# Crossbar transposes in an attention and channel-mix kernel: outputs of batches 4 to 7 pair by pair, q and k of batches 4 and 5 as well

## Chip, cores and metric

One core of one Trainium2 chip. The metric is device time in microseconds; the time before is 234.25 us, the median of three runs (233.97 to 234.29).

## The reference

Sliding-window attention with a linear distance bias over 8 batches of 8 heads (576 positions, 64 per head), then a channel mix of the attention's output with its own row before. Cut to what is computed:

```python
# q, k, v: (8, 8, 576, 64)
scores = q @ k.T / sqrt(64)
rel = i - j                       # query less key position
scores = where((rel >= 0) & (rel < 128), scores - slope[h] * abs(rel), -1e9)
attn = softmax(scores) @ v
x = attn.transpose(0, 2, 1, 3).reshape(8, 576, 512)

x_prev = x shifted down by one row (a zero row first)
xk = mu_k * x + (1 - mu_k) * x_prev
xr = mu_r * x + (1 - mu_r) * x_prev
k = relu(xk @ w_k)                # w_k: 512 x 1024
v = (k * k) @ w_v                 # w_v: 1024 x 512
out = sigmoid(xr @ w_r) * v       # w_r: 512 x 512
```

## The kernel before

The kernel doesn't call its instructions in the order in which they run. It describes each piece of work as a node with an engine, an assumed duration, its dependences, a priority and the buffers that it takes and frees; a list scheduler (`Plan.run`) then plays the program through with these durations and fixes the order on every engine. On the chip each engine runs its list in order and waits by semaphores. The scheduler also has a make-believe engine FAB, which stands for the DMA engines: `dma` and `fab` cut a transfer into pieces of about 0.25 us there, and their `lat` gives the time from issue to the first piece and from the last piece to the landing. None of these numbers is in the program itself; they set its order.

Heads go in pairs: batch b has four pairs g = 0 to 3, each 128 wide (two heads of 64). A pair passes these stations:

- Loads on GpSimd's queue, which cast to bf16: q and k into `cb` (L471, two buffers), the last 64 positions of q and k into `ts` (L461), v into `vs` and `tv`. A load waits until its buffer is free.
- q and k with the head dimension on partitions. Batches 3 to 5 do that on TensorE, two pairs at a time: `qk_some` (L1153) with 32 transposes of 64 columns (L779), and copies by ScalarE from PSUM to `qk`. Batches 1 and 2 have a like form (L1032). For batches in `XB`, which are 6 and 7, the crossbar of the DMA does it: `flip` (L474) issues eight transposes per batch on SyncE's queue (SP), each 128 x 512 from `cb` to one of two `qx` buffers. `XTT` (batches 4 to 7) does the same for the tails, `tail_flip` (L564), from `ts` to `tt`.
- Scores on TensorE (L666), exponential on ScalarE (L680), mask on VectorE (L693).
- Attend on TensorE (L724), then reciprocal (L730) and normalisation (L735) on VectorE, which writes the pair's output in bf16: to `xu` (one of three buffers), or for batches in `XO` (6 and 7) to `xb`, which holds all four pairs of a batch.
- The output with the channel on partitions, in `xt`. `out_t` (L751) does it with five TensorE transposes (L762) and one ScalarE copy. For batches in `XO`, `out_flip` (L841) waits for all four pairs and issues five crossbar transposes on SP (L847), one for each 128 positions.
- `shift` (L805) on VectorE: the difference of a row and the one before into `dl` (L822), and the two mixes xk and xr (L829).

Every one or two batches `channel_mix` (L922) takes xk and xr in column blocks of 512, 384 or 256: TensorE multiplies by `w_k` (L937), ScalarE takes relu (L944), VectorE squares (L910), TensorE multiplies by `w_r` (L955) and `w_v` (L971), VectorE multiplies the two (L976) into `ot`, and SP stores it (L1001). These blocks are laid between the attention's pieces and fill TensorE.

SP's queue holds in one order: the output stores, the tail transposes, the q and k transposes, the output transposes. An instruction that waits holds up those behind it.

Of the kernel before, what the change touches and what calls it, by code (L numbers as in the profile page):

```python
# [10 lines left out]
BF16 = mybir.dt.bfloat16  # L11
# [168 lines left out]
def kernel(  # L180
# [12 lines left out]
    nc = tc.nc  # L193

    B, H, S, D = q.shape
# [13 lines left out]

    PE, ACT, DVE, POOL, SPE, FAB, VIR = "PE", "ACT", "DVE", "POOL", "SP", "FAB", "VIR"  # L210
    NQ, NA, NX, NV, NC = 4, 4, 3, 2, 2
    XB = range(6, B)
    XO = range(6, B)
    X0 = 16
    NWARM = 90
    LOADS = 'vK23tVkabRcWw'
# [7 lines left out]
    TW = (0,)  # L224
    QUAD = 0.040
    RUN = {2: 64 * 284 / 345.0, NF: 128 * 284 / 390.0}
    FLIP = 1.25
    NO = 5
    WAIT = 1.0
    QM = 2  # L230
# [26 lines left out]
    def many(n, shape, dtype, name):  # L257
        return [cst.tile(shape, dtype, name=f"{name}{i}") for i in range(n)]
# [16 lines left out]
    at_buf = many(NA, [128, 2 * 1024 + 64], BF16, "at")  # L275
    rc_buf = many(NX, [128, 2, NJ], FP32, "rc")
    xu_buf = many(NX, [128, NJ, 2, D], BF16, "xu")
    xb_buf = many(2, [128, NJ, H, D], BF16, "xb")
    xt_buf = many(2, [128, NPO, X0 + S], BF16, "xt")
    dl_buf = many(2, [128, S], BF16, "dl")  # L280
    xk_buf = many(2, [128, NPO, SP], BF16, "xk")
    xr_buf = many(2, [128, NPO, SP], BF16, "xr")
# [25 lines left out]
    def two(h):  # L308
        return duo[h.idx]

    plan = Plan(dict(qx=2, xb=2, p2=2, p1=N1, pt=4 - N1, qk=NQ, at=NA, xu=NX, vs=NV, cb=NC, ts=2, tt=2, xt=2, dl=2, dl0=4,
                     xk=2, rl=3, kk=3, rs=4, ot=NO),
                {}, WAIT)
    LAT = {PE: 0.2, ACT: 0.22, DVE: 0.16}
# [36 lines left out]
    def virtual(key, holds):  # L351
        n = plan.add(VIR, 0.0001, 0.0001, [last.get(key)], (0,), None, holds)
        last[key] = n
        return n
# [117 lines left out]
            out=cb_buf[h.idx][:, i, r], in_=src[:, :, r]), [g]) for r in range(NF)]  # L472

    def flip(b, i, j, g):  # L474
        return dma(SPE, FLIP * RATE, 1.3, lambda e: nc.sync.dma_start_transpose(
            out=qx_buf[xbh[b].idx][:, i, :, 128 * j:128 * j + 128],
            in_=cb_buf[ch[b].idx][:, i, j].rearrange("p h d -> p (h d)")),
            [g, (cl[b][NF * i + j], 6.0)], (), [ch[b]])

    def w_load(dst, src, kb):  # L480
        return dma(POOL, kb, 0.85, lambda e: nc.gpsimd.dma_start(
# [82 lines left out]
    def tail_flip(b):  # L564
        htt, hs = Hold("tt"), th[b]
        g = plan.add(VIR, 0.0001, 0.0001, [], (0,), None, [htt])
        tth[b], ttg[b] = htt, g
        ttl[b] = [dma(SPE, FLIP * RATE, 1.3, lambda e: nc.sync.dma_start_transpose(
            out=tt_buf[htt.idx][:, :, 0:2].rearrange("p g t c -> p g (t c)"),
            in_=ts_buf[hs.idx].rearrange("p h d -> p (h d)")),  # L570
            [g] + [(x, 6.0) for x in tl[b]], (), [hs])]

    def batch_load(b, what):
        if what == "a":
# [124 lines left out]
    def attend(b, g, t0, t1, ha, deps, prio):  # L699

        nt = t1 - t0
        n_mm = sum(2 if t > 0 else 1 for t in range(t0, t1)) * 2
        hp, hx = Hold("p1" if 2 * nt * W <= 512 else "p2"), xbh_o[b] if b in XO else Hold("xu")
        rc = rc_buf[(4 * b + g) % NX]

        def xo():
            if b in XO:
                return xb_buf[hx.idx][:, t0:t1, 2 * g:2 * g + 2]
            return xu_buf[hx.idx][:, t0:t1]
        hv = vh[b]  # L710

        def a5():
            if hp.cls == "p1":
                return one(hp)[:, 0:2 * nt * W].rearrange("p (h t c) -> p h t c", h=2, c=W)
            return two(hp)[:, :, 0:nt * W].rearrange("p h (t c) -> p h t c", c=W)

        def emit(e):
            at, vs, tvb, a = at_buf[ha.idx], vs_buf[hv.idx], tv_buf[hv.idx], a5()
            for t in range(t0, t1):
                for hl in range(2):  # L720
                    us = [u for u in (t - 1, t) if u >= 0]
                    for u in us:
                        lo = 1024 * hl + BASE[u] + 128 * (t - u)
                        nc.tensor.matmul(  # L724
                            a[:, hl, t - t0], lhsT=at[:, lo:lo + 128],
                            rhs=vs[:, u, 2 * g + hl, :] if u < NF else tvb[:, 2 * g + hl],
                            start=(u == us[0]), stop=(u == t), skip_group_check=True)

        def emit_r(e):
            nc.vector.reciprocal(out=rc[:, :, 0:nt], in_=a5()[:, :, :, D])  # L730

        def emit_x(e):
            out_ = xo().rearrange("p t h d -> p h t d")
            if e == DVE:
                nc.vector.tensor_tensor(  # L735
                    out=out_, in0=a5()[:, :, :, 0:D],
                    in1=rc[:, :, 0:nt, None].to_broadcast([128, 2, nt, D]), op=ALU.mult)
                return
            for t in range(nt):
                for hl in range(2):  # L740
                    nc.scalar.activation(out=out_[:, hl, t], in_=a5()[:, hl, t, 0:D],
                                         func=AF.Copy, scale=rc[:, hl, t:t + 1])

        a = op(PE, 0.029 * n_mm, deps, prio + (0,), emit, [hp], [ha, hv])
        r = op(DVE, 0.2, [a], prio + (0,), emit_r)
        on = XU(b, g)
        r = op(on, {ACT: 0.197 * 2 * nt, DVE: dve_t(2 * nt * D)}, [r], prio + (0,), emit_x,
               [] if b in XO else [hx], [hp])
        return r, hx

    def out_t(b, g, t0, t1, hx, deps, prio, hk, ht, late=None):  # L751
# [86 lines left out]
                res.append(mix())  # L838
        return res

    def out_flip(b, rs, hx, ht):  # L841

        res = []
        for t in range(NJ):
            rows = min(128, S - 128 * t)
            n = plan.add(SPE, 1.3 * rows / 128, 0.0, rs + [virt_xt[b]], (0, len(plan.nodes)),
                         lambda e, t=t, rows=rows: nc.sync.dma_start_transpose(  # L847
                out=xt_buf[ht.idx][:, :, X0 + 128 * t:X0 + 128 * t + rows],
                in_=xb_buf[hx.idx][0:rows, t].rearrange("p h d -> p (h d)")))
            res.append(fab(SPE, 1.0 * rows / 128, n, (1.0, 0.9), [hx]))  # L850
        return res

    def tails_full(b, prio, htt, hs):
        hp = Hold("p1")
# [45 lines left out]

    of = out.rearrange("b s m -> (b s) m")

    n_hw = 39 + sum(4 if g in FT else 2 for g in range(3)) + 8 * len(XB) + len(XTT) + NJ * len(XO)
    n_split = -n_hw % 8

    def square(e, out, in_):
# [99 lines left out]

    xh, virt_x, virt_xt, xth, xbh_o = {}, {}, {}, {}, {}

    def begin(b):
        if b % 2 == 0:
# [181 lines left out]
    for b in range(1, B):  # L1194
        begin(b)
        P = b // 2
        rs = []
        if b in XO:
            xbh_o[b] = Hold("xb")
            rs.append(virtual("xb", [xbh_o[b]]))  # L1200
        htt, n_tt = tails(b, (0, b, 0, 0))
        for g in range(G):
            prio = (0, b, 0, g)
            ha = Hold("at")
            if b in XB:
                hq, y = xbh[b], xbl[b]
                pace = paced(b, g)
            else:
                pace = []
                if b in WIDE:  # L1210
                    two_q[:] = [qk_quad(b, g, NF, lambda b=b: wide_buf[ch[b].idx], cw[b][g // 2] + paced(b, g),
                                        prio, 0, Hold("qk"), True, [ch[b]])]
                elif not QM:
                    two_q[:] = [qk_full(b, g, prio)]
                elif g % QM == 0:
                    two_q[:] = qk_some(b, g, QM, prio)
                hq, y = two_q[0 if b in WIDE else g % max(QM, 1)]
            _, (m0, m1) = scores(b, g, [HALF0 + (None,), HALF1 + (htt,)], 4 * b + g < NBIAS, hq, ha,
                                 y + pace + (n_sid if b < 3 else []) + n_tt, prio, [ha], [hq, htt])
            r, hx = attend(b, g, 0, NJ, ha, [m0, m1] + vl[b] + rs[0:1], prio)  # L1220
            if b in XO:
                rs.append(r)
            elif not OM:
                xks[b, g], xrs[b, g] = out_t(b, g, 0, NJ, hx, [r], prio, xh[P], xth[b])
            else:
                two_x.append((hx, r))
                if len(two_x) < OM:
                    continue
                xs = out_some(b, g - OM + 1, [x for x, _ in two_x], [x for _, x in two_x], prio, xth[b])
                two_x.clear()  # L1230
                for j in range(g - OM + 1, g + 1):
                    xks[b, j], xrs[b, j] = shift(b, j, 0, S, xs, (0, b, 0, j), xh[P], xth[b])
        if b in XO:
            fl = out_flip(b, rs, xbh_o[b], xth[b])
            for g in range(G):
                xks[b, g], xrs[b, g] = shift(b, g, 0, S, fl, (0, b, 0, g + XD), xh[P], xth[b])
        own = lambda d: [d[b, g] for g in range(G)]
        if b % 2:
            both = [[own(d) + ([d[0, 1, g] for g in range(G)] if b == 1 else
                               [d[b - 1, g] for g in range(G)])][0] for d in (xks, xrs)]  # L1240
            channel_mix(P, 512, 896, False, both[0], both[1], 2 * b)
            channel_mix(P, 896, SP, False, own(xks), own(xrs), 2 * b + 1)
        else:
            channel_mix(P, 0, 512, False, own(xks), own(xrs), 2 * b)
# [36 lines left out]
```

## Time and profile before

| what | us |
|---|---|
| median of the runs | 234.25 |
| span of the profiled execution | 232.7 |
| TensorE busy | 226.0 |
| VectorE busy | 188.4 |
| ScalarE busy | 166.1 |
| attention of batches 4 and 5, first scores to last attend | 96.5 to 139.9 |
| first scores of batch 6 | 141.7 |
| last attend of batch 7 | 187.3 |

The span runs from the first to the last instruction of the profiled execution; the runs' time is some 1.5 us longer. The granted TensorE clock is full all through. The busiest groups are the three matrix products of the channel mix (L971, L937, L955). The two lists of transposes that the change touches on TensorE:

```profile
L762 PE MATMUL uno<-ident,xu x120: 216/219/230, 11.7 to 142.5; 128*128 128x128 bf16 x120
```

```profile
L779 PE MATMUL uno<-ident,cb x192: 186/190/200, 64.1 to 119.2; 64*128 64x64 bf16 x192
```

Each line tells of one kind of instruction: the count, the shortest, median and longest duration in ns, and the starts of the first and the last in us. Matmuls are pipelined, so the durations overlap and can't be added; what a block costs is read from the starts of the blocks around it.

And on SP's queue, out<-in, count, KB, and the median us from the issue of a transfer to its landing:

```profile
out_dram<-ot SPq DMA_DIRECT2D x32, 256.0 KB, 3.5
...
qx<-cb SPq DMA_TRANSPOSE x16, 5.7
...
xt<-xb SPq DMA_TRANSPOSE x10, 2.4
tt<-ts SPq DMA_TRANSPOSE x4, 2.5
```

### The profile page before, as it was taken

What the parts mean: (1) busy time and instruction counts of PE and PEld (TensorE: products, weight loads), DVE (VectorE), ACT (ScalarE), POOL (GpSimd) and SP (SyncE); (2) the same over time, 40 slices, a digit from 0 to 9 for tenths busy, and PEclk for the clock granted to TensorE, in tenths of its full rate; (3) what the DMA queues carried; (4) which work ended last, traced back from release to release, by engine and by line L of the source; (5) the groups of instructions that cost most, each with busy time, mean ns of one, the idle gap of its engine ahead of it and who ended that gap; (6) DMA issues with size and microseconds to landing.
All of it is one profiled execution on the core that took longest, in us unless ns stands there. A gap on an engine that the chain in (4) does not pass through costs nothing.

```text
span 232.7 us, 6483 instructions
## 1 busy us (share of the span) xinstructions
PE 226.0 (97%) x2615; PEld 138.3 (59%) x2615; DVE 188.4 (81%) x416; ACT 166.1 (71%) x302; POOL 93.6 (40%) x120
## 2 busy tenths in 40 slices
PE   8799989999999999999999999999999999999994
PEld 7476758566666756555665765555654754445462
DVE  7477998998899979989998999855779994794242
ACT  3569999969998779979798777675572926326251
POOL 8777664599873980098329817000000000000000
PEclk9999999999999999999999999999999999999999
DMA  6999999999999999199999999981332114221112
GB/s 158 183 165 188 192 165 203 175 197 180 171 159 128 151 150 168 23 107 171 203 145 94 169 181 177 190 136 60 122 70 93 45 49 101 90 92 48 66 69 90
DMA packets 120829, 30.96 MB, mean 133 GB/s; under 512 B 107736, under 2 KB 116704, under 8 KB 120800
## 3 DMA queue, kind: packets, MB, share of 16 engines
q0 software_dynamic: 96016, 16.26, 98.8%
q1 hardware_dynamic: 23040, 13.71, 25.3%
q10 hardware_dynamic: 1744, 0.59, 1.0%
q8 instruction: 20, 0.33, 0.6%
q14 instruction: 9, 0.07, 0.1%
HBM read 33.56 MB, written 9.44 MB: 185 GB/s over the span
## 4 chain that ended last, share of the span: by engine, by line
PE 87%; DMA 6%; ACT 3%; issue 1%; POOL 0%; DVE 0%; DVEq 0%; POOLq 0%
PE uno L971 27%; PE uno L937 26%; PE uno L955 13%; PE duo L666 7%; PE duo L724 7%; DMA ts<-in_k_dram 3%; DMA vs<-in_v_dram 3%; PE uno L762 3%; PE uno L779 1%; ACT qk L636 1%; PE duo L653 1%; PE uno L1032 1%; ACT rl L944 1%; PE uno L724 1%; ACT kk L908 1%
## 5 line engine op out<-in xcount | busy, mean ns | idle before, releaser
L971 PE MATMUL uno<-wv_sb,kk 128*128 128x512 bf16 (+2 forms) x296 | 71.9, 374 | 0.0
L937 PE MATMUL uno<-xk,wk_sb 128*128 128x256 bf16 (+2 forms) x416 | 69.4, 314 | 0.3 <-ACT qk L636 0.3
L680 ACT ACTIVATE at<-duo 128x1024 bf16<-128x1024 f32 (+2 forms) x68 | 64.9, 998 | 4.3 <-PE duo L666 4.2
L944 ACT ACTIVATE rl<-uno 128x256 bf16<-128x256 f32 (+2 forms) x104 | 47.9, 487 | 21.0 <-PE uno L937 19.1
L937 PEld LDWEIGHTS <-wk_sb 128*128 128x128 bf16 x416 | 39.2, 98 | 22.7 <-issue 0.7
L440 POOL DMA_DIRECT2D vs<-in_v_dram x32 | 28.4, 898 | 36.5 <-PE duo L724 28.3
L971 PEld LDWEIGHTS <-kk 128*128 128x128 bf16 x296 | 26.8, 98 | 26.7 <-issue 0.2
L693 DVE TENSOR_TENSOR at<-at,mask 128x1024 bf16<-128x1024 bf16 x56 | 37.4, 680 | 4.2 <-ACT at L680 4.0
L962 ACT ACTIVATE rs<-uno 128x512 bf16<-128x512 f32 x36 | 22.4, 621 | 24.7 <-PE uno L955 21.9
L910 DVE TENSOR_TENSOR kk<-rl 128x256 bf16<-128x256 bf16 (+2 forms) x91 | 29.9, 344 | 11.2 <-ACT rl L944 9.8
L955 PE MATMUL uno<-wr_sb,xr 128*128 128x512 bf16 x144 | 37.0, 379 | 0.8 <-DVE qk L636 0.7
L976 DVE SCALAR_TENSOR_TENSOR ot<-rs,uno 128x512 f32<-128x512 bf16 (+2 forms) x37 | 24.7, 669 | 13.7 <-PE uno L971 8.1
L724 PEld LDWEIGHTS <-at 128*128 128x128 bf16 x576 | 21.8, 98 | 5.6 <-issue 1.2
L829 DVE SCALAR_TENSOR_TENSOR xk<-dl,mu_sb,xt 128x576 bf16<-128x576 bf16 (+1 forms) x32 | 24.7, 780 | 0.2
L829 DVE SCALAR_TENSOR_TENSOR xr<-dl,mu_sb,xt 128x576 bf16<-128x576 bf16 (+1 forms) x32 | 24.3, 767 | 0.0
L636 ACT COPY qk<-uno 128x512 bf16<-128x512 bf16 (+1 forms) x43 | 22.7, 602 | 1.7 <-PE uno L1032 0.9
L955 PEld LDWEIGHTS <-xr 128*128 128x128 bf16 x144 | 13.3, 98 | 14.4 <-issue 0.7
L636 ACT COPY xt<-uno 128x576 bf16<-128x576 bf16 (+2 forms) x28 | 16.1, 584 | 5.1 <-PE uno L762 5.1
L724 PE MATMUL duo<-vs,at 128*128 128x65 bf16 x448 | 19.1, 194 | 0.0
L471 POOL DMA_DIRECT2D cb<-in_k_dram x20 | 17.8, 892 | 3.2 <-DMA vs<-in_v_dram 2.1
L471 POOL DMA_DIRECT2D cb<-in_q_dram x20 | 17.7, 916 | 1.2 <-PE duo L724 0.9
L822 DVE TENSOR_TENSOR dl<-xt 128x576 bf16<-128x576 bf16 (+1 forms) x32 | 13.7, 438 | 3.9 <-ACT xt L636 3.8
(82 smaller groups left out, 219.7 us busy)
## 6 DMA issues: line engine op xcount, KB each, us to landing
out_dram<-ot SPq DMA_DIRECT2D x32, 256.0 KB, 3.5
vs<-in_v_dram POOLq DMA_DIRECT2D x32, 128.0 KB, 7.1
cb<-in_q_dram POOLq DMA_DIRECT2D x20, 128.0 KB, 6.5
cb<-in_k_dram POOLq DMA_DIRECT2D x20, 128.0 KB, 6.2
wk_sb<-in_moe_w_k_dram POOLq DMA_DIRECT2D x2, 512.0 KB, 7.6
cb<-in_q_dram POOLq DMA_DIRECT2D x4, 256.0 KB, 9.4
cb<-in_k_dram POOLq DMA_DIRECT2D x4, 256.0 KB, 10.2
wv_sb<-in_moe_w_v_dram POOLq DMA_DIRECT2D x2, 512.0 KB, 9.6
```

The lines of the kernel that those rows point to most:

```text
L440: return dma(POOL, 256, issue_t(1024), lambda e: nc.gpsimd.dma_start(out=vs_buf[h.idx][:, j, :, 0:D], in_=v[b, :, 128 * j:128 * j + 128].r ...
L471: return [dma(POOL, 256, issue_t(1024), lambda e, r=r: nc.gpsimd.dma_start(out=cb_buf[h.idx][:, i, r], in_=src[:, :, r]), [g]) for r in ra ...
L636: (nc.scalar.copy if e == ACT else nc.vector.tensor_copy)(out=out, in_=in_)
L680: lambda e, ah=ah, w=w, hp=hp: nc.scalar.activation(out=ah(), in_=two(hp)[:, :, 0:w], func=AF.Exp, scale=float(scale)), (), [hp])
L693: nc.vector.tensor_tensor(out=a, in0=a, in1=m, op=ALU.mult)
L724: nc.tensor.matmul(a[:, hl, t - t0], lhsT=at[:, lo:lo + 128], rhs=vs[:, u, 2 * g + hl, :] if u < NF else tvb[:, 2 * g + hl], start=(u == u ...
L829: lambda e: nc.vector.scalar_tensor_tensor(out=buf[hk.idx][:, g, e0 + c0:e0 + c1], in0=dls(), scalar=mu[:, g:g + 1], in1=xc(1), op0=ALU.mu ...
L910: nc.vector.tensor_tensor(out=out, in0=in_, in1=in_, op=ALU.mult)
L937: nc.tensor.matmul(one(hp)[:, 0:n], lhsT=wk_sb[:, po, 128 * fo:128 * fo + 128], rhs=xk_buf[hx.idx][:, po, c0:c1], start=(po == 0), stop=(p ...
L944: a = op(ACT, act_t(n), [s], pr, lambda e, hp=hp, hr=hr: nc.scalar.activation(out=rl_buf[hr.idx][:, 0:n], in_=one(hp)[:, 0:n], func=AF.Rel ...
L955: nc.tensor.matmul(one(hp), lhsT=xr_buf[hx.idx][:, po, 128 * c:128 * c + 128], rhs=wr_sb[:, po], start=(po == 0), stop=(po == NPO - 1))
L971: nc.tensor.matmul(one(hv)[:, a:b], lhsT=kk_buf[hk.idx][:, fo, o:o + 128], rhs=wv_sb[:, fo, a:b], start=(fo == 0), stop=(fo == NFO - 1))
```

## The change

`XB` and `XO` both become batches 4 to 7. So q and k of batches 4 and 5 go through the crossbar, eight transposes each, in place of `qk_some`; their loads take the row order that `flip` needs. The outputs of batches 4 to 7 go through the crossbar, but no longer by batch: `out_flip` is called for each pair as soon as its normalisation has written `xu`, and issues one transpose of five 128 x 128 tiles from `xu` to the pair's part of `xt`, all 640 columns. `xb` is gone, and `xt` is widened to take the full last tile. `shift` follows each pair's own transpose. The scheduler's numbers for a transpose change too: `FLIP` (its time on FAB) from 1.25 to 0.6, the latencies around it from 1.0 and 0.9 to `FLAT` = 0.4 and 0.6; `FISSUE` and `FWAIT` are new names for 1.3 and 6.0. The number of SP transfers enters `n_hw`, which decides how many of the last output rows are stored in two halves.

```diff
-    XB = range(6, B)
-    XO = range(6, B)
+    XB = range(4, B)
+    XO = range(4, B)
...
-    FLIP = 1.25
+    FLIP = 0.6
+    FISSUE = 1.3
+    FLAT = (0.4, 0.6)
+    FWAIT = 6.0
...
-    xb_buf = many(2, [128, NJ, H, D], BF16, "xb")
-    xt_buf = many(2, [128, NPO, X0 + S], BF16, "xt")
+    xt_buf = many(2, [128, NPO, X0 + 128 * NJ], BF16, "xt")
...
     def flip(b, i, j, g):
-        return dma(SPE, FLIP * RATE, 1.3, lambda e: nc.sync.dma_start_transpose(
+        return dma(SPE, FLIP * RATE, FISSUE, lambda e: nc.sync.dma_start_transpose(
             out=qx_buf[xbh[b].idx][:, i, :, 128 * j:128 * j + 128],
             in_=cb_buf[ch[b].idx][:, i, j].rearrange("p h d -> p (h d)")),
-            [g, (cl[b][NF * i + j], 6.0)], (), [ch[b]])
+            [g, (cl[b][NF * i + j], FWAIT)], (), [ch[b]], FLAT)
...
-        hp, hx = Hold("p1" if 2 * nt * W <= 512 else "p2"), xbh_o[b] if b in XO else Hold("xu")
+        hp, hx = Hold("p1" if 2 * nt * W <= 512 else "p2"), Hold("xu")
...
-    def out_flip(b, rs, hx, ht):
-
-        res = []
-        for t in range(NJ):
-            rows = min(128, S - 128 * t)
-            n = plan.add(SPE, 1.3 * rows / 128, 0.0, rs + [virt_xt[b]], (0, len(plan.nodes)),
-                         lambda e, t=t, rows=rows: nc.sync.dma_start_transpose(
-                out=xt_buf[ht.idx][:, :, X0 + 128 * t:X0 + 128 * t + rows],
-                in_=xb_buf[hx.idx][0:rows, t].rearrange("p h d -> p (h d)")))
-            res.append(fab(SPE, 1.0 * rows / 128, n, (1.0, 0.9), [hx]))
-        return res
+    def out_flip(b, g, r, hx, ht):
+
+        n = plan.add(SPE, FISSUE, 0.0, [r, virt_xt[b]], (0, len(plan.nodes)),
+                     lambda e: nc.sync.dma_start_transpose(
+            out=xt_buf[ht.idx][:, g, X0:X0 + 128 * NJ].rearrange("p (t c) -> p t c", c=128),
+            in_=xu_buf[hx.idx].rearrange("p t h d -> p (t h d)")))
+        return [fab(SPE, FLIP * NJ / 4, n, FLAT, [hx])]
...
-    n_hw = 39 + sum(4 if g in FT else 2 for g in range(3)) + 8 * len(XB) + len(XTT) + NJ * len(XO)
+    n_hw = 39 + sum(4 if g in FT else 2 for g in range(3)) + 8 * len(XB) + len(XTT) + G * len(XO)
...
             if b in XO:
-                rs.append(r)
+                xks[b, g], xrs[b, g] = shift(b, g, 0, S, out_flip(b, g, r, hx, xth[b]),
+                                             (0, b, 0, g + XD), xh[P], xth[b])
...
-        if b in XO:
-            fl = out_flip(b, rs, xbh_o[b], xth[b])
-            for g in range(G):
-                xks[b, g], xrs[b, g] = shift(b, g, 0, S, fl, (0, b, 0, g + XD), xh[P], xth[b])
```

More of the change, by code (lines that the diff above doesn't have):

```diff
@@ L309, in two @@
         return duo[h.idx]
-    plan = Plan(dict(qx=2, xb=2, p2=2, p1=N1, pt=4 - N1, qk=NQ, at=NA, xu=NX, vs=NV, cb=NC, ts=2, tt=2, xt=2, dl=2, dl0=4,
+    plan = Plan(dict(qx=2, p2=2, p1=N1, pt=4 - N1, qk=NQ, at=NA, xu=NX, vs=NV, cb=NC, ts=2, tt=2, xt=2, dl=2, dl0=4,
                      xk=2, rl=3, kk=3, rs=4, ot=NO),
@@ L567, in tail_flip @@
         tth[b], ttg[b] = htt, g
-        ttl[b] = [dma(SPE, FLIP * RATE, 1.3, lambda e: nc.sync.dma_start_transpose(
+        ttl[b] = [dma(SPE, FLIP * RATE, FISSUE, lambda e: nc.sync.dma_start_transpose(
             out=tt_buf[htt.idx][:, :, 0:2].rearrange("p g t c -> p g (t c)"),
             in_=ts_buf[hs.idx].rearrange("p h d -> p (h d)")),
-            [g] + [(x, 6.0) for x in tl[b]], (), [hs])]
+            [g] + [(x, FWAIT) for x in tl[b]], (), [hs], FLAT)]
     def batch_load(b, what):
@@ L702, in attend @@
         n_mm = sum(2 if t > 0 else 1 for t in range(t0, t1)) * 2
-        hp, hx = Hold("p1" if 2 * nt * W <= 512 else "p2"), xbh_o[b] if b in XO else Hold("xu")
+        hp, hx = Hold("p1" if 2 * nt * W <= 512 else "p2"), Hold("xu")
         rc = rc_buf[(4 * b + g) % NX]
         def xo():
-            if b in XO:
-                return xb_buf[hx.idx][:, t0:t1, 2 * g:2 * g + 2]
             return xu_buf[hx.idx][:, t0:t1]
@@ L747, in attend @@
         r = op(on, {ACT: 0.197 * 2 * nt, DVE: dve_t(2 * nt * D)}, [r], prio + (0,), emit_x,
-               [] if b in XO else [hx], [hp])
+               [hx], [hp])
         return r, hx
@@ L1005, in channel_mix @@
                 plan.add(VIR, 0.0001, 0.0, [(y, OTL)], (0,), None, (), [ho])
-    xh, virt_x, virt_xt, xth, xbh_o = {}, {}, {}, {}, {}
+    xh, virt_x, virt_xt, xth = {}, {}, {}, {}
     def begin(b):
@@ L1196 @@
         P = b // 2
[L1197 to L1200, printed above, removed]
         htt, n_tt = tails(b, (0, b, 0, 0))
@@ L1219 @@
                                  y + pace + (n_sid if b < 3 else []) + n_tt, prio, [ha], [hq, htt])
-            r, hx = attend(b, g, 0, NJ, ha, [m0, m1] + vl[b] + rs[0:1], prio)
+            r, hx = attend(b, g, 0, NJ, ha, [m0, m1] + vl[b], prio)
             if b in XO:
-                rs.append(r)
+                xks[b, g], xrs[b, g] = shift(b, g, 0, S, out_flip(b, g, r, hx, xth[b]),
+                                             (0, b, 0, g + XD), xh[P], xth[b])
             elif not OM:
@@ L1232 @@
                     xks[b, j], xrs[b, j] = shift(b, j, 0, S, xs, (0, b, 0, j), xh[P], xth[b])
-        if b in XO:
-            fl = out_flip(b, rs, xbh_o[b], xth[b])
-            for g in range(G):
-                xks[b, g], xrs[b, g] = shift(b, g, 0, S, fl, (0, b, 0, g + XD), xh[P], xth[b])
         own = lambda d: [d[b, g] for g in range(G)]
```

## The prediction

> **What bounds the kernel now.** I read the page's head and slices first, then busy time by stage, then the chain of waits in order of time, and last the crossbar transposes of the SP queue and the VectorE timeline. The head and two of the slice lines:
>
> ```profile
> span 232.7 us, 6483 instructions
> PE 226.0 (97%) x2615; PEld 138.3 (59%) x2615; DVE 188.4 (81%) x416; ACT 166.1 (71%) x302; POOL 93.6 (40%) x120
> PE   8799989999999999999999999999999999999994
> DMA  6999999999999999199999999981332114221112
> ```
>
> TensorE (PE) has something in hand nearly always. Busy time by stage shows which other engines are near their limit. The columns are window, length, then busy us of PE, weight load, VectorE (DVE), ScalarE (ACT), GpSimd; granted clock, DMA share, GB/s:
>
> ```profile
> 95.00:140.00 45.00, 45.00 (x563) 28.28 (x562) 42.50 (x85) 38.01 (x64) 25.25 (x31) 1.00 1.70 140
> 140.00:190.00 50.00, 50.00 (x457) 28.19 (x455) 41.42 (x85) 31.13 (x51) 4.11 (x5) 1.00 0.75 108
> ```
>
> Batches 4 and 5 run in the first of these: PE has no idle time, and DVE only 2.5 us of 45. Loads are in flight through most of it. The chain of waits (start, us, what) around the end of batch 4:
>
> ```profile
> 107.50 0.47 PE uno L779 x32
> ...
> 114.64 0.28 PE uno L762 x5
> ...
> 115.46 2.71 PE uno L937 x16
> 118.17 0.55 PE duo L666 x12
> 118.72 0.65 PE uno L779 x32
> 119.36 0.97 PE uno L955 x4
> ```
>
> Piece follows piece without a gap, and the chain is on PE. Four 512-column matmuls start 0.86 us after the four before them, and 16 of 384 columns take 2.71 us, which is 0.17 us each: the pieces grow with their columns, so this is throughput and not waiting. What is taken off PE here is worth its full length, as long as PE's next work is ready.
>
> The Trainium skill ("Trainium Kernel Development and Optimization", section Performance Expectations) calls matmul busy time a bad measure, since matmuls are pipelined. By that the 97% proves nothing and the gain could be zero, the third rival below; the spacing of the pieces speaks against it.
>
> **What leaves PE.** The q and k of batches 4 and 5 go through L779 in four blocks of 32. The chain gives 0.47 us for a block between scores and 0.65 us for the one that ends beside another row mode. The blocks at 85.8 and 107.5 are 0.47 and the last 0.65; the fourth stands as the first two: 3 x 0.47 + 0.65 = 2.06. The outputs of batches 4 and 5 go through L762, eight blocks of five at 0.28 us: 2.24. Together 4.3 us.
>
> ACT loses 16 copies of 646 ns (qk) and 8 of 638 ns (xt), 15.4 us. It isn't on the chain there, so I count nothing. DVE keeps all its operations. GpSimd's loads are the same in number and order.
>
> **What is added on SP.** 16 transposes of q and k at 1.22 us of issue, and 16 output transposes of five tiles in place of ten of mostly four. The trace has no five-tile transpose: its bounds are 1.25 us (issue does not grow) and 1.57 us (5/4 of 1.254); I take 1.57: the half-height fifth transposes also take 1.25, so it isn't the rows that set it. That is 19.5 + 25.1 - 12.5 = 32 us more of issue. It lies in SP's waits for output tiles (over 100 us in all), except where the order puts something urgent behind it. Output stores stand behind it too; five output buffers cover them, and without that cover DVE would wait for a store of some 6 us beside loads. Two more of the last output rows are stored in halves, off the chain.
>
> **What replaces the path of an output pair.** Before, L762 on PE and an ACT copy lead from the normalised pair (xu) to its subtraction dl (L822) in some 2 us. Now dl waits for SP to issue and the crossbar to land. Two states stand in the trace. The output transposes of batches 6 and 7, when no load runs:
>
> ```profile
> L847 SPq DMA_TRANSPOSE xt<-xb x10: 1190/1254/1267, 166.0 to 195.9; - x10
> ...
> DMA to landing us min/median/max: 2.3/2.4/2.4
> ```
>
> And the q/k transposes of batch 7, beside the loads:
>
> ```profile
> L475 SPq DMA_TRANSPOSE qx<-cb x8: 1191/1248/2855, 132.7 to 150.9; - x8
> ...
> DMA to landing us min/median/max: 4.9/7.1/8.9
> ```
>
> The second is three times the first. So an output pair needs 0.1 + 2.4 + 0.3 = 2.8 us alone and 0.1 + 7.1 + 0.3 = 7.5 us beside loads (0.1 for SP to wake, 0.3 for the fifth tile).
>
> The Trainium skill ("DMA: Bandwidth & Descriptors", section Issuing engines are not separate DMA queues) says that DMAs from SP and GpSimd end on the same 16 engines and interleave. The trace agrees, with 2.4 against 7.1; by the rule the outputs of batches 4 and 5 are the slow kind, by the first row alone the sum would end at 230.0.
>
> **Does DVE wait for them?** The changed program's order of instructions tells what DVE does between writing a pair and subtracting it. I price that by the spacing of starts in the DVE timeline:
>
> ```profile
> 112.86 0.45 DVE L822 TENSOR_TENSOR dl<-xt 128x576 bf16<-128x576 bf16 x1
> 113.22 0.82 DVE L735 TENSOR_TENSOR xu<-duo,rc 128x640 bf16<-128x640 f32 x1
> 113.96 0.35 DVE L910 TENSOR_TENSOR kk<-rl 128x384 bf16<-128x384 bf16 x1
> 114.22 0.81 DVE L829 SCALAR_TENSOR_TENSOR xk<-dl,mu_sb,xt 128x576 bf16<-128x576 bf16 x1
> 114.95 0.62 DVE L910 TENSOR_TENSOR kk<-rl 128x384 bf16<-128x384 bf16 x2
> ```
>
> dl 0.36, xu 0.74, square 0.27, mix 0.73; likewise mask and output 0.60. Between pair and dl stand, for pairs 0 to 3, 4.1, 7.1, 4.7 and 4.6 us in batch 4 and 5.3, 5.4, 6.2 and 4.8 in batch 5; in batches 6 and 7 2.3 to 5.2. Against 2.8 almost all are covered; against 7.5 nearly all of batches 4 and 5 are short, by 0.4 to 3.4. Behind a waiting dl on DVE are the masks and normalisations of the next pairs, and PE's attend (L724) waits for the masks.
>
> How little PE can absorb, from the timeline:
>
> ```profile
> 128.67 1.28 DVE L693 TENSOR_TENSOR at<-at,mask 128x1024 bf16<-128x1024 bf16 x2
> 130.49 0.62 PE L724 MATMUL duo<-vs,at 128*128 128x65 bf16 x15
> ```
>
> The masks end at 129.95 and the attend starts at 130.49: about 0.5 us. Through the eight pairs, by hand:
>
> - Batch 4, pair 0: short by 3.4, but DVE must wait for the attend of pair 2 anyway. Landing 2.0 + 7.5 after its attend, then 1.4 of DVE work, makes 10.9 against 9.9 of PE work. 1.0 less 0.6 of cover: 0.4 lost.
> - Pairs 1 and 2: 0.4 short, and landing in the break between the loads (117.9 to 120.8 before): nothing.
> - Pair 3: lands as v of batch 6 is loaded, 7.5 against 4.6: 2.9 less 0.6: 2.3 lost.
> - Batch 5: short by 1.3 to 2.7, but PE and what follows on DVE now come 2.3 later, and the masks of its last pair are due some 17 us after its first attend either way: nothing.
> - SP's queue: behind the output of batch 5, pair 0 stand the last q/k transpose and the tail transpose of batch 6. From that attend 2.6 (to xu) + 1.6 + 1.3 + 7.1 = 12.6 us to the tails, against 12.5 of PE work before batch 6's first scores: 0.1.
>
> 0.4 + 2.3 + 0.1 = 2.8 us. The bounds: nothing (landing 2.4 everywhere; no landing can add to the gain, since PE's removed work is already counted whole), and 7.9 us (2.8 and a tail landing in 12.1 us, the longest of the loads of cb: 5.1 for 0.1). 2.8 follows from 7.1, the row nearest in state.
>
> **Sum.** On the profiled execution 232.7 - 4.3 + 2.8 = 231.2 of span. The median of the runs is 234.25, 1.55 more, which I carry along: 232.75, so **232.8 us**.
>
> **Rivals.**
>
> - *The crossbar hides everything*: landings near 2.4 us, or DVE's cover longer than counted. 234.25 - 4.3 = 230.0. For it: batches 6 and 7 already do so. Against: their outputs come when no load runs, and 10 to 23 us before dl.
> - *Slower: the tails of batch 6 come late.* The place is SP's queue, where the tail transpose stands behind an output that is only written at 2.6 us after batch 5's first attend. It decides from a landing of 7.0 us on, one for one; transposes and loads slow each other (loads of cb land in 6.6 at the median and 12.1 at worst, the latter beside transposes). Between the longest transposes, 8.9, and 12.1 the wait is 1.9 to 5.1, in the middle 3.5: 234.25 - 4.3 + 2.8 + 3.5 = 236.3. For it: the tail transpose at 126.5 took 8.1. Against: before, it was awaited only 7 us after landing, so a late DVE also makes PE late and gives it time.
> - *PE's work is hidden anyway* and the time stays: 234.2.
>
> **Chances.** Forecast 0.38, everything hidden 0.18, slower by the tails 0.34, no gain 0.10. About 0.2% (0.5 us) is what this kernel's measurement can tell from no change. The forecast spreads some 1.5 us around 232.8, so I count 0.30 of its 0.38 as faster, 0.04 as the same and 0.04 as slower; with 0.18 and 0.34 and the last split 0/0.08/0.02: faster 0.48, same 0.12, slower 0.40. The range takes in both rivals: 229.8 to 237.8. The forecast's own is 231.3 to 234.3.
>
> **What would show it.** PE work down by 4.3 us (L779 64 left, L762 80 left). Idle time on PE between 100 and 145 us, near none before: 2.8 us if I am right, released by masks or normalisations on DVE, and DVE idle before dl released by the DMA of xt. Output transposes at 100 to 150 us landing in about 7 us, later ones in under 3. The forecast is wrong if those land in 3 us, or if PE waits longest at the first scores of batch 6 (then for tt or qx).

## The result, and the profile after

| | us |
|---|---|
| before, median (range) | 234.20 (233.97 to 234.29) |
| after, median (range) | 244.69 (243.96 to 244.88) |
| ratio after to before, 95% interval | 1.0442 (1.0426 to 1.0458) |
| span of the profiled execution, before and after | 232.7 and 242.9 |

The change makes the kernel 10.5 us slower. The forecast was 232.8, and 244.69 lies above the whole range of 229.8 to 237.8. All medians here and below are of executions in the chip's faster state; one execution of e15 was in the slower one and is left out of its median.

The head and three slice lines of the page after:

```profile
span 242.9 us, 6201 instructions
PE 226.2 (93%) x2447; PEld 135.5 (56%) x2447; DVE 187.7 (77%) x416; ACT 155.2 (64%) x278; POOL 93.7 (39%) x120
PE   8899989999999999999589299999999999999994
PEclk9999999999999999999799989999999999999999
DMA  7999999999999999999999999994652704031122
```

PE has 168 matmuls less, yet its busy time is the same. Slices 20, 21 and 23 (115 to 140 us) have holes, and the granted clock falls at the first and behind the last. The DMA slices stay full to 164 us, before to 151, and the break that they had at 93 to 99 us is gone.

Busy time by stage, columns as before (PE, weight load, DVE, ACT, GpSimd, clock, DMA share, GB/s):

```profile
95.00:140.00 45.00, 36.10 (x319) 20.14 (x315) 31.41 (x62) 22.09 (x35) 23.84 (x28) 0.95 1.77 168
140.00:190.00 50.00, 49.12 (x454) 27.45 (x453) 45.03 (x90) 29.93 (x46) 5.57 (x7) 0.98 1.04 137
```

Before, PE was busy through all 45 us of the first stage; now 8.9 us of it are idle. The sum, on the spans: -4.3 for PE's removed work, +9.9 of idle time on PE (13.4 in all against 3.5), +3.4 for the clock (0.986 over the span of 242.9) make +9.0, of the 10.2 measured; where the other 1.2 us come from stays open.

What the idle time waited for. The view of waits (engine and line, what ended the wait: us in total, times, longest), then the chain around batch 4 (start, us, what):

```profile
DVE dl L822 <- DMA xt<-xu: 10.2, 5, 4.4
DVE xu L735 <- DMA xt<-xu: 2.1, 1, 2.1
```

```profile
106.81 0.60 DVE ot L972
107.42 8.47 DMA xt<-xu
115.91 0.47 DVE dl L822
...
118.13 1.17 PE uno L933 x4
119.30 7.28 DMA xt<-xu
126.62 0.04 issue
126.67 0.84 DVE xu L735
127.56 8.85 DMA xt<-xu
136.45 0.04 issue
136.50 0.47 DVE dl L822
```

Three landings of batch 4's own pairs stand in the chain one behind the other: pair 0, pair 2, pair 3. The second holds up a normalisation, not a subtraction: pair 3 wants the buffer that pair 2's transpose is still reading. The program's order shows why. There are three `xu` buffers, but the scheduler takes the lowest that it thinks free, and it thinks that a transpose lands 0.6 us after its last piece. Of 16 transposes 10 read the first buffer, 6 the second, none the third, and pairs 2 and 3 of batch 4 and pair 0 of batch 5 all use the first.

The transfers themselves. First the output transposes in the changed kernel, then the loads of `cb` (KB each, median us to landing), after and then before:

```profile
L844 SPq DMA_TRANSPOSE xt<-xu x16: 1199/1222/2642, 107.4 to 203.2; - x16
...
DMA to landing us min/median/max: 2.4/4.4/8.6
```

```profile
cb<-in_q_dram POOLq DMA_DIRECT2D x20, 128.0 KB, 10.8
cb<-in_k_dram POOLq DMA_DIRECT2D x20, 128.0 KB, 12.8
```

```profile
cb<-in_q_dram POOLq DMA_DIRECT2D x20, 128.0 KB, 6.5
cb<-in_k_dram POOLq DMA_DIRECT2D x20, 128.0 KB, 6.2
```

Five tiles issue in the time of four (1222 ns at the median). Landings are 7.2 to 8.9 us for all that were issued up to 146 us, then 5.4 and less, and these loads take about twice as long as before.

The clock behind the first hole, in windows of 2 us (same columns):

```profile
116.00:118.00 2.00, 0.00 (x0) 0.00 (x0) 1.96 (x5) 0.41 (x2) 1.34 (x2) 1.00 1.60 208
118.00:120.00 2.00, 1.87 (x6) 0.86 (x6) 2.00 (x6) 1.34 (x4) 0.00 (x0) 0.53 1.42 251
120.00:122.00 2.00, 2.00 (x7) 0.72 (x6) 1.71 (x4) 0.69 (x2) 0.00 (x0) 0.62 1.73 159
122.00:124.00 2.00, 2.00 (x26) 1.19 (x25) 1.05 (x3) 0.00 (x0) 1.22 (x2) 1.00 2.36 148
```

PE stood for 2.45 us and then ran at 0.53 and 0.62 of its clock in two windows: the stop costs 0.47 x 1.87 + 0.38 x 2.00 = 1.6 us more. In e10 below, a stop of 2.96 us left the clock at 1.00, so the length of a stop alone doesn't decide. The Trainium skill ("TensorE: Matmul & The Clock Gate", section Part 1: The HAM clock gate) says that the clock is halved after an idle window of about 3.4 us, and that this window runs free. Here 2.45 us were enough, which is shorter than such a window; that the window runs free could be why stops of like length differ, but no run here shows that.

### The profile page after: what moved, and what is told of

It reads as the page before. It is cut to its first block, busy times and chain, and to the rows that moved or that the text cites. A ratio compares the mean times of both kernels' runs of the same rounds, so it can differ in the third digit from the quotient of the medians.

```text
span 242.9 us, 6201 instructions
## 1 busy us (share of the span) xinstructions
PE 226.2 (93%) x2447; PEld 135.5 (56%) x2447; DVE 187.7 (77%) x416; ACT 155.2 (64%) x278; POOL 93.7 (39%) x120
## 4 chain that ended last, share of the span: by engine, by line
PE 65%; DMA 18%; DVE 7%; ACT 3%; POOL 3%; issue 2%; DVEq 0%; POOLq 0%; ACTq 0%; SPq 0%
PE uno L967 21%; PE uno L933 19%; DMA xt<-xu 15%; PE uno L951 11%; PE duo L668 5%; PE duo L724 5%; DMA ts<-in_k_dram 3%; PE uno L762 2%; DVE xk L829 1%; DVE at L695 1%; DVE ot L972 1%; POOL qx L438 1%; DVE dl L822 1%; ACT rl L940 1%; ACT qk L638 1%
## 5 line engine op out<-in xcount | busy, mean ns | idle before, releaser
L933 PE MATMUL uno<-xk,wk_sb 128*128 128x256 bf16 (+2 forms) x416 | 72.3, 319 | 8.1 <-DVE ot L972 4.6
L933 PEld LDWEIGHTS <-wk_sb 128*128 128x128 bf16 x416 | 39.7, 99 | 32.0 <-issue 9.8
L951 PE MATMUL uno<-wr_sb,xr 128*128 128x512 bf16 x144 | 37.8, 386 | 1.4 <-DVE qk L638 0.7
L735 DVE TENSOR_TENSOR xu<-duo,rc 128x640 bf16<-128x640 f32 x28 | 22.9, 819 | 2.3 <-DMA xt<-xu 2.1
L822 DVE TENSOR_TENSOR dl<-xt 128x576 bf16<-128x576 bf16 (+1 forms) x32 | 14.0, 439 | 13.5 <-DMA xt<-xu 10.2
L951 PEld LDWEIGHTS <-xr 128*128 128x128 bf16 x144 | 13.9, 99 | 16.3 <-issue 2.4
L638 ACT COPY qk<-uno 128x512 bf16<-128x512 bf16 (+1 forms) x27 | 13.9, 567 | 1.9 <-PE uno L1075 1.0
```

Of the source, the lines that this page charges most:

```text
L933: nc.tensor.matmul(one(hp)[:, 0:n], lhsT=wk_sb[:, po, 128 * fo:128 * fo + 128], rhs=xk_buf[hx.idx][:, po, c0:c1], start=(po == 0), stop=(p ...
L951: nc.tensor.matmul(one(hp), lhsT=xr_buf[hx.idx][:, po, 128 * c:128 * c + 128], rhs=wr_sb[:, po], start=(po == 0), stop=(po == NPO - 1))
```

## The experiments

| run | what | us, median | ratio to before (95%) |
|---|---|---|---|
| e1 | q and k of 4, 5 by the crossbar; outputs of 6, 7 only | 239.1 | 1.0183 (1.0142 to 1.0224) |
| e2 | outputs of 4 to 7; q and k of 6, 7 only | 245.9 | 1.0496 (1.0462 to 1.0529) |
| e3 | pairwise form for 6, 7 only | 237.7 | 1.0168 (1.0119 to 1.0218) |
| e4 | whole change, eight xu buffers in turn | 244.2 | 1.0407 (1.0367 to 1.0447) |
| e5 | e3, 5.5 us told for an output transpose | 234.3 | 0.9992 (0.9976 to 1.0008) |
| e6 | e2, the same | 239.8 | 1.0230 (1.0198 to 1.0263) |
| e7 | whole change, the same | 244.9 | 1.0433 (1.0370 to 1.0497) |
| e8 | before, 16 idle transposes added | 250.1 | 1.0667 (1.0644 to 1.0691) |
| e9 | e8, output tiles in turn | 236.5 | 1.0103 (1.0080 to 1.0126) |
| e10 | e6, eight xu, xu and output tiles in turn | 237.1 | 1.0128 (1.0106 to 1.0151) |
| e11 | e7, the same | 243.7 | 1.0417 (1.0389 to 1.0446) |
| e12 | before, loads of 5 to 7 cut to an eighth | 234.4 | 0.9989 (0.9971 to 1.0007) |
| e13 | whole change, the same | 231.7 | 0.9894 (0.9851 to 0.9936) |
| e14 | e10, q and k transposes planned late | 234.2 | 0.9997 (0.9963 to 1.0030) |
| e15 | e11, the same | 237.2 | 1.0118 (1.0065 to 1.0170) |
| e16 | e14, 8 us told for every transpose | 238.3 | 1.0166 (1.0112 to 1.0221) |
| e17 | e15, 8 us told, and 16 from load to transpose | 241.8 | 1.0306 (1.0257 to 1.0355) |
| e18 | e14, three xu, lowest free again | 240.9 | 1.0273 (1.0232 to 1.0313) |

**The parts alone (e1 to e4).** Which part loses, and do the three buffers do it?

```diff
-    XO = range(4, B)
+    XO = range(6, B)          # e1 and e3
-    XB = range(4, B)
+    XB = range(6, B)          # e2 and e3
```

In e4 `NX` is 8 in place of 3 and the buffers are taken in turn.

> The changed kernel with XO = 6 and 7: outputs of batches 4 and 5 go back to TensorE (L762) and ScalarE, q and k of batches 4 to 7 stay with the crossbar. Theory A (the loss comes from the output transposes, whose landing beside loads of 7 to 8.9 us stands on VectorE's path): the 2.06 us of the q/k blocks are gained and the stops go, about 232, and VectorE waits for no DMA of xt before 150 us. Rival B (the extra q/k transposes lengthen the loads and all landings, and that is the loss): still slow, 239 to 245, with loads of cb landing in 12 to 18 us and TensorE idle before first scores.

> The changed kernel with XB = 6 and 7: q and k of batches 4 and 5 go back to TensorE, outputs of batches 4 to 7 stay pair by pair on the crossbar. Theory A: most of the loss stays, 238 to 244, with chain pieces DMA xt<-xu of 7 us at 100 to 150 us. Rival B: the 2.24 us of L762 are gained or nearly, 231 to 235, as loads land in 6 to 7 us again and the output transposes in under 5.

> The changed kernel with XB = XO = 6 and 7: only the outputs of 6 and 7 differ from before (pair by pair from xu, the scheduler's new numbers). Theory A and B: no load runs beside most of them, so within 1 us of before, 233.5 to 235.5. If it is 2 us slower or more, the way from xu itself (three buffers, a wait per pair) or the new numbers cost something without any loads.

> The changed kernel with eight xu buffers taken in turn in place of three with the lowest free one: a normalisation no longer has to wait for an output transpose that still reads its buffer. Theory C (the buffer makes a ring: transpose, normalisation, transpose, some 8 us each turn): the waits of xu for DMA xt<-xu go and 3 to 6 us come back, 238.5 to 241.5. Theory A alone (only the subtraction dl waits): within 1.5 us of the changed kernel, 243 to 246.

Each part loses alone: e1 comes out at the lower end of rival B's range, with loads of `cb` at some 9 us in place of the 12 to 18 expected, and e2 a little above theory A's. In e2 VectorE waits 12.2 us for `xt` at subtractions, against 10.2 in the change. In e3 there is a single wait of this kind, VectorE's 3.86 us before the first subtraction of batch 6. That wait, and SP's queue before it (start, us, line, what):

```profile
DVE dl L822 <- DMA xt<-xu: 3.9, 1, 3.9
```

```profile
145.12 4.81 SPq L477 DMA_TRANSPOSE qx<-cb  x3
150.10 2.56 SPq L570 DMA_TRANSPOSE tt<-ts  x1
152.76 1.32 SPq L844 DMA_TRANSPOSE xt<-xu  x1
```

The pair was written at 149.0, but SP was at work on the q, k and tail transposes of batch 7 and issued it at 152.8; it landed 4.0 us later. So of the 7.8 us from writing to landing about half is queue and half landing. PE stood for 1.98 us and then ran below full clock (0.76 and 0.50 in two windows of 2 us), and the time rose by 3.5. Two of the four runs kept a clock of 0.999 and 1.00 and took 237.5 all the same, so the clock isn't what makes this loss. The pairwise form thus costs 3.5 even for the two batches that I had called covered, and e1 and e2 have it too (in e1 the same subtraction waits 5.2 us). In e4 the wait for `xu` is gone, but those at the subtraction grow to 12.6: more buffers alone move the wait.

**The order (e5 to e7).** One number that only the scheduler sees:

```diff
-        return [fab(SPE, FLIP * NJ / 4, n, FLAT, [hx])]
+        return [fab(SPE, FLIP * NJ / 4, n, (0.4, 5.5), [hx])]
```

> The pairwise form for batches 6 and 7 alone, with one number told to the scheduler changed: an output transpose lands 5.5 us after its last piece instead of 0.6. It changes only the order of the instructions (VectorE has 5.6 to 9.5 us of other work between a pair's normalisation and its subtraction in batch 6). Theory O (the loss is an order that leaves too little between pair and dl, and what PE's stop then costs): VectorE's 3.86 us before the first dl of batch 6 goes and PE's stop with it, 233.5 to 235. Rival D (the DMA engines are shared, so transposes and loads slow each other and a wait comes in any order): 237 or more, with a wait of 2 us or more for xt at another dl.

> Outputs of batches 4 to 7 by the crossbar, q and k of batches 4 and 5 on PE, with the same 5.5 us told to the scheduler. Theory O: 6.3 to 11.1 us of VectorE's work cover landings of some 7.7, so most of the waits of 3.5, 4.6, 2.3 us go: 232 to 236. Rival D: landings and loads grow further or waits stay, 241 or more (245.9 without the number).

> The whole change with the same 5.5 us told to the scheduler. Theory O: 231 to 236 (PE has 4.3 us less to do than before; what is left are loads that land 10 us late and the q and k transposes). Rival D: 240 or more, with waits for xt of together 6 us or more.

For batches 6 and 7 the order was the whole loss: the wait is gone, and the time is that of before. For the outputs of batches 4 to 7 (e6) it is worth 6.1 us of 11.7, between the two expectations, and then the buffer waits; for the whole change (e7) it is worth nothing. SP's queue in e6 shows what a pair meets now (start, us, line, what; the last line is from its view of waits):

```profile
116.71 10.06 SPq L477 DMA_TRANSPOSE qx<-cb  x6
126.87 1.37 SPq L844 DMA_TRANSPOSE xt<-xu  x1
```

```profile
DVE xu L735 <- DMA xt<-xu: 8.6, 3, 7.5
```

Pair 3 of batch 4 was written at 123.8 and issued at 126.9, behind six q and k transposes of batch 6 that took 10 us to issue; it landed at 135.6, and the next pair's normalisation waited for its buffer.

**Idle transposes (e8, e9).** Contention by itself: the kernel before, where the tail transposes of batches 4 and 5 are followed by eight more each that nobody reads. The order of the four other engines is unchanged.

```diff
+            for n in range(2 * NF if b in (4, 5) else 0):
+                nc.sync.dma_start_transpose(
+                    out=xb_buf[1][:, n % NJ].rearrange("p (g a) d -> p g (a d)", g=G),
+                    in_=cb_buf[ch[b].idx][:, n // NF, n % NF].rearrange("p h d -> p (h d)"))
```

> The kernel before, with eight transposes of cb added behind the tail transpose of each of batches 4 and 5; they write a buffer that nobody reads, and the order on the four other engines is that of before. So only SP and the DMA engines get more. Theory O: loads land at 9 us or more in place of 6.6, but none is late: within 0.5 us of before. Rival D: 236 or more, with waits of GpSimd's loads, tails or output stores on PE or VectorE.

> The run before (16 idle transposes in the kernel before), but the five output tiles are taken in turn; in the kernel before the scheduler takes the lowest free one, and 31 of 36 stores use two of the five. The order on every engine is unchanged. Theory Q (the 15.7 us of the run before were SP's queue: transposes that wait and issue slowly hold up the stores, and VectorE waits for one of two output tiles): 234 to 237, no wait for out_dram above 2 us. Rival D (loads and transposes slow each other on the DMA engines): 242 or more, with waits on loads or tails.

The time rose by 15.7 us, though nobody waits for them. SP's queue in e8, and the wait that comes of it:

```profile
101.17 1.22 SPq L570 DMA_TRANSPOSE tt<-ts  x1
102.49 13.18 SPq L574 DMA_TRANSPOSE xb<-cb  x8
115.72 7.73 SPq L1008 DMA_DIRECT2D out_dram<-ot  x3
```

```profile
DVE ot L983 <- DMA out_dram<-ot: 12.3, 1, 12.3
PE uno L944 <- DVE ot L983: 12.1, 1, 12.1
```

Eight transposes hold the queue for 13 us; the store behind them is issued at 115.7 and lands 6.6 us later, and VectorE waits 12.3 us for that output tile. There are five, but the scheduler again takes the lowest free one, and 32 of the 36 tiles go through two of them (the 31 in the expectation missed one). Taken in turn (e9), the same transposes cost 2.35 us, of which 1.47 is PE at the first scores of batch 6:

```profile
PE duo L679 <- DMA tt<-ts: 1.5, 1, 1.5
```

The number of e8 is rival D's, and the way is mostly theory Q's: 13.6 of the 15.7 us go when no tile has to wait behind the queue. The 2.35 that stay are not all that sharing costs, though, since it also lengthens the queue: those eight issues took 12.3 us in all, against 9.8 at 1.22 each. And the loads pay. The q and k loads of batch 6 in e9, where only idle transposes were added and every engine's order is that of before, and then in the kernel before:

```profile
DMA to landing us min/median/max: 7.8/10.8/14.7
```

```profile
DMA to landing us min/median/max: 6.2/6.8/7.2
```

**Buffers in turn (e10, e11, e18).** `xu` eight times, and `xu` and output tiles in turn:

```diff
-            return min(free) if free else None
+            k, n = self.ring[h.cls]
+            return min(free, key=lambda a: (a - k) % n)
...
-    NQ, NA, NX, NV, NC = 4, 4, 3, 2, 2
+    NQ, NA, NX, NV, NC = 4, 4, 8, 2, 2
```

> Outputs of batches 4 to 7 by the crossbar, q and k of 4 and 5 on PE, 5.5 us told to the scheduler, and eight xu buffers in place of three, these and the five output tiles taken in turn. Theory B (after the order, the buffers are what waits: VectorE's 7.5 us for xu, held by transposes that SP issues late): 233 to 236. Rival D: 238 or more, the wait back at dl or on loads (239.8 without the buffers).

> The whole change with 5.5 us told to the scheduler, eight xu buffers, and these and the output tiles taken in turn. Theory B: VectorE's waits for xu (8.9 us) and output tiles (5.3 us) go, 232 to 236. Rival D: 240 or more, with waits on loads that land at 12 to 18 us, or on xt at dl (244.9 without the buffers).

> The run with outputs alone at 5.5 and 12 us (234.2), with its three xu buffers again and the lowest free xu buffer and output tile taken, as in the change. If the buffers are needed beside the order: 236 to 239, with waits for xu or output tiles. If the order does it alone: 234 to 235.

e10 gains 2.7 us on e6, which is between its two expectations, and e11 1.2 on e7. e18 undoes the buffers in the best version of the outputs (e14, below) and loses 6.8 us, with one wait of 6.4 us for `xu`: beside a longer order the buffers are a cause of their own. The longer order without them (e6) leaves 5.4 us of loss; buffers without the longer order were tried only in the whole change (e4), where they were worth 0.5. In e10 four waits of together 7.8 us at the subtraction are left, behind q and k transposes in SP's queue: pair 0 of batch 6 is written at 151.2, issued at 154.2 and lands at 164.0. In e11 the waits are elsewhere, at the first scores of batches 5 to 7:

```profile
PE duo L674 <- DMA qx<-cb: 6.1, 3, 2.6
PE duo L674 <- DMA tt<-ts: 2.8, 3, 1.1
```

**Loads cut (e12, e13).** Order, buffers and queue exactly as in the two kernels; only the loads of q, k and v of batches 5 to 7 move 16 of 128 partitions, so the rest of that input is left out:

```diff
-            out=cb_buf[h.idx][:, i, r], in_=src[:, :, r]), [g]) for r in range(NF)]
+            out=cb_buf[h.idx][0:few(b), i, r], in_=src[0:few(b), :, r]), [g]) for r in range(NF)]
```

(`few(b)` is 16 from batch 5 on; v in the same way.)

> The kernel before, with the loads of q, k and v of batches 5 to 7 cut to 16 of their 128 partitions (the rest keeps older values, so a part of the input is left out; the tails are loaded whole). The order on every engine is that of before. It is the base for the run with the change. PE has no idle time to give there: 233.5 to 234.5 under every theory.

> The changed kernel with the same loads cut to 16 of 128 partitions from batch 5 on (that part of the input is left out); order, buffers and every transpose are those of the change. Rival D (loads and transposes slow each other): output transposes land in 2.4 to 4 us, few waits are left, 229.5 to 233, so the 4.3 us of PE's work show. Theory O (the order, two or three buffers and SP's queue alone would do it): 238 or more with landings still near 7.

The kernel before stays at 234.4, the changed one falls from 244.7 to 231.7. Its output transposes and its only waits for them:

```profile
L847 SPq DMA_TRANSPOSE xt<-xu x16: 1199/1227/2395, 106.8 to 190.3; - x16
...
DMA to landing us min/median/max: 2.4/2.5/4.1
```

```profile
DVE dl L825 <- DMA xt<-xu: 3.2, 2, 1.7
```

With the same order, the same two buffers and the same queue, 13.0 us go when the loads go, and 2.7 us of PE's 4.3 show. The transposes are not slow by themselves: loads slow them, as here, and they slow loads, as in e9. (The cut also makes GpSimd's issues shorter, 0.56 us for 0.88 at the median, so it isn't the engines' share alone that changes.)

**SP's order, and how far it can be stretched (e14 to e17).** Loads told to land 12 us ahead of a q or k transpose in place of 6, and these transposes 5.5 us after their last piece (those of the tails likewise):

```diff
-    FWAIT = 6.0
+    FWAIT = 12.0
...
-            [g, (cl[b][NF * i + j], FWAIT)], (), [ch[b]], FLAT)
+            [g, (cl[b][NF * i + j], FWAIT)], (), [ch[b]], (0.4, 5.5))
```

e16 puts 8.0 for 5.5, e17 that and 16 for 12.

> The run with outputs of batches 4 to 7 by the crossbar, 5.5 us told and all buffers (237.1), with two more numbers told to the scheduler: loads land 12 us before a q or k transpose in place of 6, and these land 5.5 us after their last piece. SP's queue then has two or three q and k transposes ahead of an output, not six. Theory Q (what is left there is outputs behind other transposes in SP's queue, 2 to 6 us late): 233 to 235.5. Rival D: 236.5 or more, with waits on other landings of 8 us or more.

> The whole change with all of these numbers and buffers (243.7 without the last two). Theory Q: 236 or less. Rival D (the transfers of 79 to 176 us fill the DMA engines): 240 or more, the waits again at the first scores of batches 6 and 7 for qx and tt, loads at 12 to 18 us.

> Outputs of batches 4 to 7 by the crossbar as in the run before (234.2), with 8.0 us in place of 5.5 told for every transpose (they landed at 7 to 9). Theory O (what was left is an order still too short by some 2 us): 232 to 233.7, faster than before. Rival D: 234 or more; the further an order is stretched, the more it waits elsewhere.

> The whole change with all buffers, 8.0 us told for every transpose and 16 us from a load to its transpose (loads landed at 10 to 18). Theory O: 233 or less, since PE has 4.3 us less to do. Rival D: 236 or more.

The outputs alone now take 234.2, as before the change; one wait of 2.3 us at a subtraction is left. The whole change (e15) comes down from 243.7 to 237.2, between its two expectations, with runs from 236.1 to 238.5. Telling more (e16) takes away every wait at a subtraction and is 4.1 us slower again: the last subtraction of batch 7 moves from 202.3 to 208.5 us, and PE waits for the mixes of the last block:

```profile
L939 PE MATMUL uno<-xk,wk_sb 128*128 128x256 bf16 (+2 forms) x412 | 69.5, 313 | 4.0 <-DVE xk L835 3.4 <-ACT qk L644 0.3 <-issue 0.2
```

e17 has the same at 210 to 214 (2.8 us), and PE's waits of 3.5 us at 136 to 141. No version with all its loads beats the kernel before. Two things stay open: where e14 gives back its 2.2 us of PE's work beyond that wait, since some 30 of PE's records are missing in that trace; and how much of e15's 2.9 us is sharing on the DMA engines and how much an order that still doesn't fit.

## Why the prediction was wrong

The step that failed is "What replaces the path of an output pair", with its walk through the eight pairs: it gave 2.8 us (bounds 0 and 7.9; by its own terms the upper one is 0.4 + 2.3 + 5.1 = 7.8). Measured by the run with the outputs alone it is 13.9: 245.9 less 234.2, plus the 2.24 of PE's work that went; in the whole change it is 10.5 + 4.3 = 14.8. It took the landing beside loads rightly and went wrong in what hangs on it: the queue ahead of a pair, the loads that the transposes slow, and the buffers that they hold. By its parts:

- **Removed work: right.** PE's 168 transposes are gone. Between the two kernels with cut loads (e12 and e13, both at full clock) PE is busy for 223.9 and 219.8 us, 4.1 less where the forecast was 4.3; 2.7 of them show in the time. The third rival, that PE's work is hidden anyway, falls with that.
- **Landing: right in size.** 7.1 was forecast beside loads, and 7.2 to 8.9 measured; later ones in 2.4 to 5.4, where I said under 3. The growth of issue with five tiles (1.57 us) was wrong: 1.22. It changed nothing.
- **"Batch 4, pair 0: 0.4 lost": mis-sized.** VectorE waited 2.70 and PE stood 2.45 us. The landing took 8.47, and SP, at work on q and k transposes, issued it 1.4 us after the pair was written, where I had put 0.1.
- **"Pairs 1 and 2 ... landing in the break between the loads: nothing": wrong.** There is no break any more, because the q and k loads of batch 6 take 12.2 to 16.6 us where they took 6.2 to 7.2. I let the loads slow the transposes, and not the transposes the loads. Pair 2 also held the one buffer that pair 3 needed (2.14 us on VectorE, 1.21 on PE); I had not looked which buffers the program's order uses.
- **"Pair 3: 2.3 lost": the place was right, the size not.** 4.44 on VectorE and 4.65 on PE.
- **"Batch 5: nothing": small, as it came out.** 0.13 and 1.20 us on VectorE. PE was by then late by more than I thought; that this is why is not tested.
- **"Batches 6 and 7: almost all are covered": wrong.** One pair of batch 6 alone cost 3.5 us (e3): written 3.8 us before SP could issue it, and 4.0 us in landing.
- **"Five output buffers cover them": wrong as a reason.** 34 of the 36 tiles go through two of the five. In the change itself this cost nothing large, in e1 4.0 us of VectorE's waits and in e8 nearly all.
- **The clock** was not in the sum: 3.4 us, a third of the whole loss, come from half clock behind PE's stops. The loss doesn't need it, though: in e2 three of four runs kept a clock of 0.998 or more and lost 11 to 12 us.

The slower rival had the right sign and the right queue but the wrong place: PE's longest waits were not at the first scores of batch 6. Those waits came only when order and buffers were mended (e11), and in the kernel before with idle transposes (e9). Its general part, that transposes and loads slow each other, is what e13 and e9 show.

A rule that bears on the change: the Trainium skill ("VectorE: DVE Perf Modes", section Rules for kernel authors) advises TensorE for a 128x128 transpose if the result may go to PSUM, and the crossbar otherwise. The runs agree: five tiles took 0.28 us of PE, and 7.2 to 8.9 us by the crossbar beside loads, of which those of q and k of batch 6 landed 6 to 10 us later themselves. In e14 the two ways take the same time.

## What to carry to other kernels

A transfer that is added beside others has three prices, not one: its own landing, what it adds to the landings of the others, and the issue time that it puts ahead of everything behind it in an in-order queue (eight transposes were 13 us in e8). Before counting on "there are n buffers", read from the program's order how many are used; an allocator that takes the lowest free one, with latencies told too short, makes two of five. And tell a scheduler the landing as it is under load: 5.5 us for 0.6 was worth 6 us here (e2 to e6), but 8 us took 4 back at the end (e14 to e16), so it is a number to be tried, not to be made safe.

## What the runs showed of the hardware

- A crossbar transpose of 128 x 512 or 128 x 640 landed in 2.4 us with no load beside it and in 7 to 9 us beside loads; with the loads cut (e13) the output transposes landed in 2.5 at the median.
- Loads pay as much, which I had not expected: the q and k loads of batch 6, 128 KB each, landed in 6.2 to 7.2 us before, in 12.2 to 16.6 in the change and in 7.8 to 14.7 beside idle transposes (e9).
- The issue of a transpose on SP took 1.22 us at the median whether it had four tiles or five, and now and then 1.9 to 2.9 us (2.89 for the sixth of eight in e8); no run isolates why.
- Behind stops of PE of 1.98 us (e3) and 2.45 us the granted clock was 0.50 to 0.89 in two or three windows of 2 us, which adds up to some 3.4 us at half clock each time; behind one of 2.96 us (e10) it stayed at 1.00.
